# Turning x for the first stage: squares of 32 on VectorE and a way through DRAM in place of TensorE

## The chip, the cores and the metric

The kernel runs on one core of a Trainium2 chip. The metric is the device time of one execution in microseconds (us); a kernel's time is the median of several runs. The core's engines are TensorE (PE in the profile, its weight loads PEld), VectorE (DVE), ScalarE (ACT), GpSimd (POOL) and SyncE (SP), which issues nearly all the DMAs. Each engine works through its own instructions in a fixed order; an instruction that waits holds back all that stand behind it on its engine.

## The reference

```python
x = A_x                                   # 1 x 2048 x 576, float32
mod = (silu(c) @ w_mod).reshape(1, 6, 1, 576)
sa, ca, ga, sb, cb, gb = (mod[:, i] for i in range(6))
h = layernorm(x) * (1 + ca) + sa
q, k, v = heads(h @ A_wqkv)               # 32 heads of 18
pq, pk = phi(q), phi(k)                   # phi(t) = (t + 1 if t > 0 else exp(t)) + 1e-6
kv, z = einsum("bhsd,bhse->bhde", pk, v), einsum("bhsd->bhd", pk)
o = einsum("bhqd,bhde->bhqe", pq, kv) / (einsum("bhqd,bhd->bhq", pq, z) + 1e-6)
x = x + ga * (o @ A_wo)
h = layernorm(x) * (1 + cb) + sb
x = x + gb * (silu(h @ B_w1) @ B_w2)      # B_w1 576 x 4608
```

## The kernel before

The 2048 rows are 16 tiles of 128 rows, in four blocks (`tb` = 0 to 3) of four tiles. The first stage, about the first 205 us, makes k, v and half of q for all tiles and sums `kv` and `z` over them. The later stages (attention output, second layernorm, MLP) fill the remaining time and are the same instructions in both kernels.

A product with h needs h with its 576 columns on the partitions, that is, turned. So each block goes through these steps. `load_x` brings four tiles of x by DMA (L278, tiles `xt`). `LayerNorm.stats` (L190, L191), `finish` (L195, L196 on POOL, L199) and `normalise` (L205 on ACT, L207 on DVE) normalise the rows in place; `normalise` works twice per tile, since the last 64 columns are also written a second time, to columns 576 to 639. `turn(tb, k)` then turns chunk k, for k = 0 to 4 (four chunks of 128 columns, and a fifth that holds the last 64 columns twice): `transpose_chunk` issues four TensorE transposes of 128x128 (L228) into the PSUM bank `psT`, `modulate` (L213, ACT) scales and shifts from `psT` into `h32`, and `split_h` makes the two parts that the products read: `hT` high by a cast on ACT (L219), `hT` low by a subtraction on DVE (L135). `hT` has two buffers, one block each.

The loop over tiles t = 0 to 15 puts TensorE's work into this order, for tile t of block tb: `k_proj(t)`, a turned chunk, `v_proj(t)`, a turned chunk, `kv_mm(t - 1)`, `q_proj`, a turned chunk. The chunks of block tb + 1 are turned in tiles 2 and 3 of block tb, three and two of them; tile 0 of the next block is the first to read them. `q_proj` runs in tiles 1 to 7 (two of them in tile 1). I call the instructions of tile t for k, v and q: k3, v3, q3 and so on. TensorE's order is the order of the program.

The products for k, v and q go into a pair of PSUM buffers `psK` (`ps2`, two of them) in turn: k3, v3, q3, k4, ... So q3 can begin when k3's buffer has been read, and k4 when v3's has. k3 is read by ACT (`e`, L342) and DVE (`a`, L347); v3 by three pairs of ACT (`vx`, L599) and DVE (`vx`, L135) instructions.

The table `FIRST` names for DVE, ACT, POOL and SP the order of the first stage's instructions, and `arrange` fixes them in this order. `mod_piece` makes further rows of `mod` in the meantime from `w_mod` (L284 loads, L557 and L559 on DVE); its results are wanted in tiles 5 and 8. The weights of q wait in `accb[2]` and `accb[3]`, which are later the accumulators of blocks 2 and 3, until ACT and POOL have split them into `wq` (L327, L332, L334). Block 0 is handled apart, in halves (`turn_half` and L421 turn its tiles 2 and 3), in both kernels alike.

Of the kernel before, what the change touches and what calls it, by code (L numbers as in the profile page):

```python
# [9 lines left out]
F32 = mybir.dt.float32  # L10
# [6 lines left out]
P = 128  # L17
# [5 lines left out]
def kernel(ctx: ExitStack, tc, A_x, A_wqkv, A_wo, B_x, B_w1, B_w2, c, w_mod, out):  # L23
# [32 lines left out]
    def behind(instructions):  # L56

        with ExitStack() as order:
# [36 lines left out]

    FIRST = {
        "DVE": """
            2 1 4-5 0 3 6-7 9-10 8 11-23 26 24-25 28 27 29-30 43 31-38 40 44 46-47 39 45 48-49 41-42 51 50 53-54 52
            55 60 56 61-62 68 57 69 71-72 70 73-75 77-78 76 79-80 86-88 63-64 81 58 65 82 84 66 83 67 89 85 59 90
            148-149 91-92 150 93-94 96 95 151 97 152 98-100 153 101-105 107 106 108-111 125-126 128-129 127 130  # L100
            112-113 131-132 134-135 133 136-137 114-115 138-139 141 116 140 142 117-124 143-147 154 182-184 155-156
            185 158 157 186 159 162 160-161 187 222-225 163-165 226 166-167 169 168 170-173 192-193 195-196 194 197
            174 198-199 201-202 175 200 203-204 176-177 205-206 208 178 207 209 179-181 188-191 210-214 216 215 217
            220 218-219 221 227-228 230 229 231 234 232-233 235-258
        """,
        "Activation": """
            0-4 6-7 5 8-10 13 11-12 14-19 21 20 22-25 27 26 28-29 31 30 32 39-40 36 33 37 41-42 48 38 50 34 52 43-44
            46 58 45 47 49 51 59 53 60 54 56 55 57 61 35 62-63 65-66 64 67 70 68 71 69 72-75 77-78 76 79-80 82 81
            83-86 93 95 94 87 96 88-92 97-102 104-105 103 106 109-110 107-108 111-114 116-117 115 118-119 121 120
            122-125 132 134 133 126 135 127-131 136-139 141-142 140 143 146-147 144-145 148-150 152-153 151 154  # L110
            157-158 155-156 159-178
        """,
        "Pool": """
            0-1 3-4 2 6-7 5 8-20
        """,
        "SP": """
            0-33 38-42 47-49 34-37 50-56 43-46
        """,
    }

    def arrange(orders, start):
        for engine, text in orders.items():
            traced = [i for i in nc.cur_bb.bb.instructions[start:] if i.engine == getattr(mybir.EngineType, engine)
                      and not isinstance(i, (mybir.BassTilePoolBoundary, mybir.InstTileManualSchedule))]
# [14 lines left out]
    dram = ctx.enter_context(tc.tile_pool(name="dram", bufs=1, space=bass.MemoryType.DRAM))  # L139
# [5 lines left out]
    pa = tc.alloc_tile_pool(name="pa", bufs=1)  # L145
# [6 lines left out]
    cols = {n: const.tile([P, KC + 1, 2], F32, name=f"col_{n}") for n in ("a", "b")}  # L152
# [5 lines left out]
    accb = [accp.tile([P, 4, D], F32, name=f"acc{b}") for b in range(NB)]  # L158
# [4 lines left out]
    hT = [hTa.tile([P, 2 * KC + 2, 512], F32R, name="hT")]  # L163
# [13 lines left out]
    class LayerNorm:  # L177
# [23 lines left out]
        def normalise(self, i, xt, r, eng):  # L201
            for o, lo, hi in ((D, KC * P, D), (0, 0, D)):
                dst, src, rstd = xt[:, o : o + hi - lo], r[:, lo:hi], self.rstd[:, i : i + 1]
                if eng is A:
                    A.activation(dst, src, AF.Identity, bias=self.nm[:, i : i + 1], scale=rstd)  # L205
                else:
                    V.tensor_scalar(dst, src, self.mv[:, i, 0:1], rstd, op0=ALU.subtract, op1=ALU.mult)  # L207

    def modulate(ps, cidx, hT, col, h32, eng):

        shift, scale = col[:, cidx, 0:1], col[:, cidx, 1:2]
        if eng is A:
            A.activation(h32, ps, AF.Identity, bias=shift, scale=scale)  # L213
        else:
            V.tensor_scalar(h32, ps, scale, shift, op0=ALU.mult, op1=ALU.add)

    def split_h(ps, cidx, hT, col, h32):
        hi, lo = (cidx, KC + cidx) if cidx < KC else (2 * KC, 2 * KC + 1)
        return A.copy(hT[:, hi, :], h32), sub_hi(hT[:, lo, :], h32, hT[:, hi, :])  # L219

    def modulate_split(*chunk):

        modulate(*chunk, A)
        return split_h(*chunk)

    def transpose_chunk(xt, cidx, ps):
        for i in range(4):
            T.transpose(ps[:, i * P : (i + 1) * P], xt[i][:, cidx * P : (cidx + 1) * P], ident)  # L228
# [39 lines left out]
    def psT():  # L268
        t = psA.tile([P, 512], F32, name="psT")
        return t  # L270
# [2 lines left out]
        t = psA.tile([P, 2, 512], F32, name="psK", bufs=2)  # L273
        return t

    def load_x(tb, i):
        xt = pa.tile([P, DX], F32, name="xt", bufs=4)
        nc.sync.dma_start(xt[:, :D], x[(tb * 4 + i) * P : (tb * 4 + i + 1) * P, :])  # L278
        return xt

    def load_mod(dst, piece, k):
        kp = P if k < KC else 64
# [23 lines left out]
    xts = [load_x(0, i) for i in range(2)]  # L306
# [6 lines left out]
    xts += [load_x(0, i) for i in range(2, 4)]  # L313
    load_w(0, [KC])
    x0s = xts
    for j in (1, 2):
# [112 lines left out]
    def turn_half():  # L429

        pT = rooms(psT())
        turn_tiles(pT, (2, 3), START)
        for k in START:
            modulate_split(*half_args(1, k, pT))
# [194 lines left out]
        return ts  # L629

    def turn(tb, k):
        ps = psT()
        transpose_chunk(xts, k, ps)
        h32 = pa.tile([P, 512], F32, name="h32")
        modulate_split(ps, k, hT[tb], cols["a"], h32)

    QB = NT // 2
    qs = iter(range(NT))
    if True:
        for t in range(NT):  # L640
# [45 lines left out]
    with tc.manual_schedule(engines={mybir.EngineType.PE}):  # L686
# [4 lines left out]

        mp = pa.tile([P, DX], F32, name="xt", bufs=4)
# [10 lines left out]
        kvm = pa.tile([P, 2 * DX], F32, name="tmod")  # L705
        G.memset(kvm, 0.0)

        kvs = pa.tile([P, DX], F32, name="xt", bufs=4)[:, : NHC * HG].rearrange("p (j d) -> p j d", j=NHC)
        ku = pa.tile([P, DX], F32, name="xt", bufs=4)
# [40 lines left out]
        for j in range(KC + 1):  # L750
            psm = ps2()
            parts = [(cc, 0 if cc == j + 1 else 1) for cc in (j, j + 1) if cc < NHC]
# [7 lines left out]
            if j in (0, 2):  # L760
                r = rooms[j // 2]
# [806 lines left out]
```

## Time and profile before

| | |
|---|---|
| time, median of 3 runs | 1155.94 us (1155.23 to 1156.3) |
| the profiled execution | 1155.44 us, its span 1153.7 us |
| granted TensorE clock | 1.00 |
| TensorE busy | 1133.2 us, 98% of the span |
| VectorE busy | 974.8 us, 84% |
| ScalarE busy | 531.2 us, 46% |
| GpSimd busy | 658.3 us, 57% |
| TensorE transposes of x in blocks 1 to 3 (L228, `psT`) | 60, from 51.5 to 168.5 us |

Times in the profile run from the start of the span. A group's row names line, engine, operation, tiles (output<-inputs), shape and count, then busy time in all and the mean of one in ns, then the idle time of the engine before it and what ended it. A row of the timeline has start, length, engine, line, operation, tiles, shape and count.

### The profile page before, as it was taken

What the parts mean: (1) busy time and instruction counts of PE and PEld (TensorE: products, weight loads), DVE (VectorE), ACT (ScalarE), POOL (GpSimd) and SP (SyncE); (2) the same over time, 40 slices, a digit from 0 to 9 for tenths busy, and PEclk for the clock granted to TensorE, in tenths of its full rate; (3) what the DMA queues carried; (4) which work ended last, traced back from release to release, by engine and by line L of the source; (5) the groups of instructions that cost most, each with busy time, mean ns of one, the idle gap of its engine ahead of it and who ended that gap; (6) DMA issues with size and microseconds to landing.
All of it is one profiled execution on the core that took longest, in us unless ns stands there. A gap on an engine that the chain in (4) does not pass through costs nothing.

```text
span 1153.7 us, 19489 instructions
## 1 busy us (share of the span) xinstructions
PE 1133.2 (98%) x7159; PEld 1046.4 (91%) x7159; DVE 974.8 (84%) x1552; ACT 531.2 (46%) x1086; POOL 658.3 (57%) x748
## 2 busy tenths in 40 slices
PE   6999999999999999999999999999999999999998
PEld 4999999899998889999999999999999999999998
DVE  6876643577797999999999999999999999999996
ACT  4743442336655545444444444454454444444441
POOL 3300000264624686775776677667757767776786
PEclk9999999999999999999999999999999999999999
DMA  9522100123258976968869769779688697697674
GB/s 289 152 83 78 42 1 1 44 73 124 72 207 298 377 268 257 352 260 314 312 248 352 275 251 351 273 255 359 261 304 321 251 351 271 254 343 277 254 305 154
DMA packets 58318, 268.60 MB, mean 233 GB/s; under 512 B 5548, under 2 KB 21424, under 8 KB 35184
## 3 DMA queue, kind: packets, MB, share of 16 engines
q1 hardware_dynamic: 58052, 267.06, 63.3%
q8 instruction: 57, 0.93, 0.3%
q10 hardware_dynamic: 172, 0.30, 0.1%
q14 instruction: 37, 0.30, 0.1%
HBM read 250.56 MB, written 16.78 MB: 232 GB/s over the span
## 4 chain that ended last, share of the span: by engine, by line
PE 95%; DMA 3%; ACT 1%; DVE 1%; issue 0%; SPq 0%; ACTq 0%
PE up L1299 33%; PE down L1372 32%; PE psK L243 13%; PE big L243 7%; PE small L862 2%; PE big L873 2%; PE kvp L613 2%; DMA acc<-in_A_wqkv_dram 1%; DMA hT<-in_w_mod_dram 1%; PE psK L756 1%; PE big L788 1%; DMA room<-hd 1%; PE small L228 1%; PE psT L228 1%; PE up L1402 1%; PE down L1402 1%
## 5 line engine op out<-in xcount | busy, mean ns | idle before, releaser
L1380 DVE TENSOR_TENSOR acc<-down,acc 128x576 f32<-128x576 f32 x330 | 246.2, 753 | 14.1 <-PE down L1372 4.1
L1299 PE MATMUL up<-hT,w 128*128 128x512 f32 x916 | 240.3, 391 | 0.0
L1299 PEld LDWEIGHTS up<-hT,w 128*128 128x128 f32 x916 | 164.5, 188 | 25.7
L1334 POOL TENSOR_TENSOR s<-f,f 128x256 f32<-128x256 f32 x66 | 51.9, 786 | 163.9 <-ACT f L1315 163.9
L1372 PE MATMUL down<-w,hc 128*128 128x288 f32 x792 | 120.7, 294 | 0.0
L1372 PE MATMUL down<-w,hb 128*128 128x288 f32 x792 | 120.6, 294 | 0.0
L1372 PEld LDWEIGHTS down<-w,hb 128*128 128x128 f32 x792 | 113.6, 188 | 5.9 <-DVE U L1380 0.3
L1372 PEld LDWEIGHTS down<-w,hc 128*128 128x128 f32 x792 | 113.6, 188 | 5.6
L1380 DVE TENSOR_TENSOR U<-down,U 128x576 f32<-128x576 f32 x132 | 99.4, 753 | 17.9 <-PE down L1372 15.6
L135 DVE TENSOR_TENSOR w<-v,w 128x288 fp32r<-128x288 f32 (+1 forms) x170 | 111.7, 666 | 0.1
L243 PE MATMUL psK<-w,hT 128*128 128x256 f32 (+1 forms) x638 | 103.9, 298 | 0.0
L1299 PE MATMUL up<-room,w 128*128 128x512 f32 x348 | 93.2, 396 | 1.1 <-DMA room<-hd 1.1
L243 PEld LDWEIGHTS psK<-w,hT 128*128 128x128 f32 x638 | 91.7, 189 | 0.3 <-DVE acc L347 0.2
L1353 POOL TENSOR_TENSOR hc<-s,hc 128x512 fp32r<-128x512 f32 x66 | 89.5, 1355 | 0.0
L1315 ACT ACTIVATE f<-f 128x512 f32<-128x512 f32 x102 | 64.3, 631 | 47.8 <-DVE f L1320 25.4
L1318 DVE TENSOR_TENSOR f<-up,p 128x512 f32<-128x512 f32 x102 | 69.6, 683 | 14.7 <-PE up L1299 10.0
L196 POOL TENSOR_TENSOR rstd<-ve,neghalf 128x4 f32<-128x4 f32 (+3 forms) x10 | 9.7, 968 | 121.1 <-DVE ve L195 120.0
L1299 PEld LDWEIGHTS up<-room,w 128*128 128x128 f32 x348 | 62.4, 188 | 12.4 <-DVE f L1320 1.6
L1042 ACT CAST w<-v 128x288 fp32r<-128x288 f32 x85 | 36.6, 434 | 76.7 <-PE down L1372 55.2
L1338 POOL TENSOR_TENSOR f<-f,s 128x256 f32<-128x256 f32 x66 | 50.9, 771 | 34.1 <-DVE hb L1353 28.5
L1372 PE MATMUL down<-w,hd 128*128 128x288 f32 x396 | 63.2, 295 | 0.0
L1372 PE MATMUL down<-w,he 128*128 128x288 f32 x396 | 63.1, 295 | 0.0
(306 smaller groups left out, 2534.7 us busy)
## 6 DMA issues: line engine op xcount, KB each, us to landing
hT<-hd SPq DMA_DIRECT2D x66, 1280.0 KB, 5.9
hT<-hd SPq DMA_DIRECT2D x45, 1024.0 KB, 5.5
room<-hd SPq DMA_DIRECT2D x35, 1280.0 KB, 5.5
room<-hd SPq DMA_DIRECT2D x20, 1024.0 KB, 5.3
v<-in_B_w_dram SPq DMA_DIRECT2D x17, 576.0 KB, 6.9
v<-in_B_w_dram SPq DMA_DIRECT2D x17, 512.0 KB, 7.3
hd<-S SPq DMA_DIRECT2D x6, 1024.0 KB, 3.8
xt<-in_A_x_dram SPq DMA_DIRECT2D x16, 288.0 KB, 3.8
```

The lines of the kernel that those rows point to most:

```text
L135: return V.tensor_sub(lo, full, f32(hi))
L228: T.transpose(ps[:, i * P : (i + 1) * P], xt[i][:, cidx * P : (cidx + 1) * P], ident)
L243: T.matmul(ps, xpart(a), wpart(b), start=n == 0, stop=n == len(XW) - 1)
L1042: A.copy(self.w2[n][:, 0], src)
L1299: T.matmul(ps, left, right, start=first and m == 0, stop=m == len(seq) - 1, skip_group_check=True)
L1315: A.activation(self.f[i, k], self.f[i, k], AF.Silu)
L1318: V.tensor_add(f, self.bank[bank[1]], self.p1)
L1334: G.tensor_add(self.s[:, 0:1], half(i, 0, 1), half(i, 1, 1))
L1338: G.tensor_sub(half(i, 1, 0), half(i, 1, 0), self.s[:, 1:2])
L1353: eng.tensor_sub(t[:, :, 1, :], src, f32(t[:, :, 0, :]))
L1372: T.matmul(ps[:, p, :HALF], self.a[i, n][:, u, p * P : (p + 1) * P], self.w.w2[n][:, v], start=n in (1, 5, 7, 6) and j == 0, stop=j == 2, ...
L1380: V.tensor_add(dst, ps[:, :, :HALF], dst)
```

## The change

For blocks 1 to 3 TensorE's transposes go. The rows of a block are dealt anew: partition 32a + j of tile t holds row 128a + 32t + j (`load_block`, four DMAs of 32 partitions by 4 rows). `turn_block` turns each tile of the normalised block in squares of 32 on VectorE, into `sq`, which lies in `accb[3]`; four DMAs write `sq` to DRAM, 32 partitions each, in runs of 128 numbers (512 bytes); eight DMAs read it back with 2048-byte runs, four of 32 partitions by 4 runs into `xT` in `accb[2]` and four of 32 partitions by one run into the fifth chunk. `turn` then only modulates, in place, from SBUF, and splits as before. The block's four x tiles are one buffer. Block 1's load stands after `turn_half`, and the double 64 columns need no second normalisation. The orders of `FIRST` are new for DVE, ACT, POOL and SP.

```diff
     FIRST = {
...
-    def load_x(tb, i):
-        xt = pa.tile([P, DX], F32, name="xt", bufs=4)
-        nc.sync.dma_start(xt[:, :D], x[(tb * 4 + i) * P : (tb * 4 + i + 1) * P, :])
+    def rows4():
+        t = pa.tile([P, 4, DX], F32, name="xt")
+        return t
+
+    def load_x(i):
+        xt = x0[:, i]
+        nc.sync.dma_start(xt[:, :D], x[i * P : (i + 1) * P, :])
         return xt
+    def load_block(tb):
+        xx = rows4()
+        for a in range(4):
+            src = x[tb * 512 + a * P : tb * 512 + (a + 1) * P, :].rearrange("(t j) d -> j t d", t=4)
+            nc.sync.dma_start(xx[32 * a : 32 * a + 32, :, :D], src)
+        return xx
+
+    def turn_block(tb, xx):
+        sq = accb[NB - 1].rearrange("p a d -> p (a d)").rearrange("p (f q) -> p f q", q=P)
+        for t in range(4):
+            V.transpose(sq[:, :, 32 * t : 32 * t + 32], xx[:, t, :D].rearrange("p (f i) -> p f i", i=32))
+        room = dram.tile([32, D // 32, 4, P], F32, name=f"turned{tb}")
+        for a in range(4):
+            nc.sync.dma_start(room[:, :, a, :], sq[32 * a : 32 * a + 32])
+        xT = accb[NB - 2].rearrange("p a d -> p (a d)")[:, : KC * 512].rearrange("p (c q) -> p c q", c=KC)
+        tail = pa.tile([P, 512], F32, name="h32")
+        src = room.rearrange("i f a q -> i f (a q)")
+        for b in range(4):
+            nc.sync.dma_start(xT[32 * b : 32 * b + 32], src[:, b : 4 * KC : 4])
+        for b in range(4):
+            nc.sync.dma_start(tail[32 * b : 32 * b + 32], src[:, 4 * KC + b % 2])
+        return [xT[:, k] for k in range(KC)] + [tail]
...
     def turn(tb, k):
-        ps = psT()
-        transpose_chunk(xts, k, ps)
-        h32 = pa.tile([P, 512], F32, name="h32")
-        modulate_split(ps, k, hT[tb], cols["a"], h32)
+        modulate_split(xT[k], k, hT[tb], cols["a"], xT[k])
...
-            if i == 0 and more:
-                xts = [load_x(tb + 1, j) for j in range(4)]
+            if i == 0 and more and t > 0:
+                xx = load_block(tb + 1)
...
                 for j in range(4):
-                    ln.stats(j, xts[j])
+                    ln.stats(j, xx[:, j, :D])
                 ln.finish()
                 for j in range(4):
-                    ln.normalise(j, xts[j], xts[j], A if j % 2 else V)
+                    ln.normalise(j, xx[:, j], xx[:, j], A if j % 2 else V, ((0, 0, D),))
+                xT = turn_block(tb + 1, xx)
...
                 turn_half()
+                xx = load_block(1)
```

More of the change, by code (lines that the diff above doesn't have):

```diff
@@ L97 @@
         "DVE": """
[L98 to L102, printed above, removed]
@@ L103 @@
-            174 198-199 201-202 175 200 203-204 176-177 205-206 208 178 207 209 179-181 188-191 210-214 216 215 217
-            220 218-219 221 227-228 230 229 231 234 232-233 235-258
+            2 1 4-5 0 3 6-7 9-10 8 11-14 17 15 18 16 19 22 20-21 26 23-25 28 27 29 43-44 46-47 45 48-49 31-35 51
+            36-37 30 38 40 39 41-42 50 53-54 52 55 60 56 61 57 62 58 88 63 89 64 90 65-69 71-72 70 73-75 77-78 76
+            79-80 91 81-87 93 59 92 94-96 152 99-100 97 101 103-104 98 102 106 105 109 113 110 107 111 153 112 108
@@ new lines @@
+            127-128 130 114 131 115 129 132-134 136 116 137 117 135 138-139 154 119 118 120 140 155 121 141-143 122
+            144-146 156 124 123 157 125 147-148 126 149-151 158 186-187 196-197 199-200 159-160 198 161 201 162-163
+            202 164 203 165 205-206 188 166-167 204 207 169 208 168 173 177 189 209-211 170-171 212 172 174 213 175
+            214 176 215 190-191 228 178-179 229-231 180-185 192 222 226 232 193-194 227 195 236 216 240 217-221
+            223-225 233-235 237-239 241-264
@@ L105 @@
         """,
         "Activation": """
[L107 to L110, printed above, removed]
@@ L111 @@
-            157-158 155-156 159-178
+            0-4 6-7 5 8-10 13 11-12 14-17 21 18 20 29 31 19 30 32 22-25 27-28 26 41-43 39 36 33 40 37 48 50 38 34 52
+            44 46 45 47 56 49 57 51 58 53 35 59 54-55 60-61 65 62 66-67 70 63 68 64 71 69 75 73 80 72 76 81 77-79 74
+            82-87 91-92 88-89 93 90 94-98 100 105 99 101 108 102 106 103 112 104 117 109 113 118 107 128 110 129 111
+            114-116 119-124 135 140 125 136 142 141 146 151 126 143 147 127 152 130-134 137-139 144-145 148-150
@@ L112 @@
+            153-172
         """,
         "Pool": """
-            0-1 3-4 2 6-7 5 8-20
+            0-1 3-4 2 6-7 5 8-12 15-17 13-14 18-20
         """,
         "SP": """
-            0-33 38-42 47-49 34-37 50-56 43-46
+            0-33 62 34-45 63 46-49 64-66 71-72 50-53 67-70 54-57 73 58-61 74-75 88-91 76-87 92
         """,
@@ L123, in arrange @@
             traced = [i for i in nc.cur_bb.bb.instructions[start:] if i.engine == getattr(mybir.EngineType, engine)
-                      and not isinstance(i, (mybir.BassTilePoolBoundary, mybir.InstTileManualSchedule))]
+                      and not isinstance(i, (mybir.BassTilePoolBoundary, mybir.InstTileManualSchedule, mybir.InstRegisterMove))]
             before = None
@@ L199, in finish, with normalise @@
             V.scalar_tensor_tensor(nm, self.mv[:, a:b, 0], -1.0, rstd, op0=ALU.mult, op1=ALU.mult)
-        def normalise(self, i, xt, r, eng):
-            for o, lo, hi in ((D, KC * P, D), (0, 0, D)):
+        def normalise(self, i, xt, r, eng, parts=((D, KC * P, D), (0, 0, D))):
+            for o, lo, hi in parts:
                 dst, src, rstd = xt[:, o : o + hi - lo], r[:, lo:hi], self.rstd[:, i : i + 1]
@@ L304, in load_w @@
             load_rows(acc[5 * j + k], A_wqkv[:, ((j + 1) % 3) * D : ((j + 1) % 3 + 1) * D], k)
-    xts = [load_x(0, i) for i in range(2)]
+    x0 = rows4()
+    xts = [load_x(i) for i in range(2)]
     for a in range(2):
@@ L312 @@
     load_w(0, range(HEAD, KC))
-    xts += [load_x(0, i) for i in range(2, 4)]
+    xts += [load_x(i) for i in range(2, 4)]
     load_w(0, [KC])
@@ L689 @@
         kv_mm(NT - 1)
-        mp = pa.tile([P, DX], F32, name="xt", bufs=4)
+        rest = rows4()
+        mp = rest[:, 0]
         mask, pick = mp[:, :HG], mp[:, P : 2 * P]
@@ L706 @@
         G.memset(kvm, 0.0)
-        kvs = pa.tile([P, DX], F32, name="xt", bufs=4)[:, : NHC * HG].rearrange("p (j d) -> p j d", j=NHC)
-        ku = pa.tile([P, DX], F32, name="xt", bufs=4)
+        kvs = rest[:, 1, : NHC * HG].rearrange("p (j d) -> p j d", j=NHC)
+        ku = rest[:, 2]
         kvu = ku[:, : NHC * HG].rearrange("p (j d) -> p j d", j=NHC)
```

## The prediction

> **What bounds the kernel now.** I read the page's head, its chain, then the busy time by stretches of the first stage, since only that stage is changed.
>
> ```profile
> span 1153.7 us, 19489 instructions
> ...
> PE 1133.2 (98%) x7159; PEld 1046.4 (91%) x7159; DVE 974.8 (84%) x1552; ACT 531.2 (46%) x1086; POOL 658.3 (57%) x748
> ...
> PE 95%; DMA 3%; ACT 1%; DVE 1%; issue 0%; SPq 0%; ACTq 0%
> ...
> 35.00:75.00 40.00, 40.00 (x307) 39.79 (x306) 32.41 (x67) 22.12 (x46) 6.73 (x5) 1.00 0.52 155
> 75.00:126.00 51.00, 50.38 (x384) 49.82 (x383) 34.10 (x59) 19.53 (x37) 1.02 (x1) 1.00 0.17 46
> 126.00:170.00 44.00, 43.23 (x331) 42.86 (x330) 23.11 (x50) 19.38 (x37) 3.40 (x6) 1.00 0.08 27
> ```
>
> The last three rows give, after the length, the busy time of PE, PEld, DVE, ACT, POOL, then granted clock, DMA share and GB/s. TensorE has no idle time from 35 to 75 us and loses 0.6 and 0.8 us in the next two stretches, at the full clock. ACT is busy half of the time, DVE four fifths in the first stretch and about half in the third. So work taken from TensorE here is time, as long as nobody makes TensorE wait instead. Later stages are the same instructions with TensorE at 98% of the whole span; a shift of the first stage passes through to the end.
>
> **What goes.** The transposes are 60 instructions:
>
> ```profile
> L228 PE MATMUL psT<-ident,xt 128*128 128x128 f32 x60 | 9.0, 272 | 0.0
> ...
> 47.80 0.43 PE L243 MATMUL psK<-w,hT 128*128 128x288 f32 x2
> 75.03 0.43 PE L243 MATMUL psK<-w,hT 128*128 128x288 f32 x2
> 87.40 0.43 PE L243 MATMUL psK<-w,hT 128*128 128x288 f32 x2
> 102.73 0.51 PE L243 MATMUL psK<-w,hT 128*128 128x288 f32 x2
> 129.81 0.43 PE L243 MATMUL psK<-w,hT 128*128 128x288 f32 x2
> 150.23 0.43 PE L243 MATMUL psK<-w,hT 128*128 128x288 f32 x2
> 169.79 0.42 PE L243 MATMUL psK<-w,hT 128*128 128x288 f32 x2
> 187.17 0.43 PE L243 MATMUL psK<-w,hT 128*128 128x288 f32 x2
> ```
>
> 9.0 us is the time that they were in flight; what they cost is seen from the pace. The rows of the timeline are the starts of k2, k4, k5, k6, k8, k10, k12 and k14. A tile with q and no transposes (t = 4) takes 87.40 - 75.03 = 12.37 us. Tiles 2 and 3, with five chunks turned, take 27.23: 2.49 above two such tiles. Tiles 6 and 7 take 27.08: 2.34 above. Tiles 10 and 11 take 19.56 against 17.38 for tiles 12 and 13: 2.18. The sum is 7.0 us. The changed kernel's TensorE order is the old one without these 60, nothing added. That the change leaves them in is thus excluded.
>
> **What comes: DVE and ACT.** Per block DVE gets four turns of 128x576, and drops two normalisations of 64 columns; ACT drops two as well and now modulates from SBUF. No row shows such a turn.
>
> ```profile
> L207 DVE TENSOR_SCALAR xt<-xt,mv,rstd 128x576 f32<-128x576 f32 x6 | 3.3, 573 | 0.0
> L135 DVE TENSOR_TENSOR pk<-a,pk 128x576 fp32r<-128x576 f32 x16 | 12.3, 768 | 5.8 <-ACT pk L363 5.0
> L559 DVE SCALAR_TENSOR_TENSOR tmod<-raw,sc,tmod 128x1152 f32<-128x1152 f32 x6 | 8.5, 1414 | 0.1
> ```
>
> Bounds for one turn: 573 ns, the quickest row of that size, and 1414 ns, two passes of it. I take 768, a full pass between SBUF tiles. Twelve turns are 9.2 us of DVE time, beside TensorE where DVE has 7.6 us free of 40, 17 of 51 and 21 of 44. It counts only as a link in the chain below. ACT modulating from SBUF I leave at its old price (778 ns below); it can be no gain for TensorE.
>
> **What comes: a chain through DRAM.** In the old kernel a chunk goes from TensorE to `hT` in about 2 us. Now a block is loaded, normalised, turned, written and read back before anything of it can be modulated, and SP issues 16 further small DMAs per block less four old ones. The DMA rows:
>
> ```profile
> 69.97 1.75 SPq L278 DMA_DIRECT2D xt<-in_A_x_dram  x4
> ...
> xt<-in_A_x_dram SPq DMA_DIRECT2D x4, 288.0 KB, 4.8
> ...
> 12.57 0.55 SPq L249 DMA_DIRECT2D acc<-in_A_wqkv_dram  x1
> ...
> GB/s 184 251 218 251 218 218 201 302 352 302 218 168 218 251 184 151 218 235 218 302 302 419 385 419 352 419 386 402 385 402 402 352 386 318 251 184 151 235 251 218
> ```
>
> Four x loads of 288 KB on 128 partitions take 1.75 us to issue and 4.8 us (median) to land: the last starts about 1.4 us in and lands 5 to 6.2 us after the first issue. I take 5.3. The new transfers reach 32 partitions each, and the last row shows what fewer partitions do: it is the rate from 17.5 to 23 us in 40 slices. The first 20, in which the 64-partition loads (L249, L250) come through the queue behind one another, have a mean of 233 GB/s, the 14 after them, with 128 partitions, 381. I take 233 for 32 partitions too: 1.18 MB (4 x 288 KB) then takes 5.1 us instead of 3.1, the four main reads (1.05 MB) 4.5 instead of 2.8. So a load or a write is 5.3 + 2.0 = 7.3 us, the reads 5.3 - 0.3 + 1.7 = 6.7. The lower bound is 5.3 and 5.0, as with 128 partitions. The upper bound, from rows of 64 partitions at their slowest (151 GB/s), is 7.8 us of data instead of 5.1: 10.0 and 9.2.
>
> [...]
>
> **Block 1, link by link.** Rows for the links:
>
> ```profile
> 35.02 0.49 PE L421 MATMUL kvp<-ident,xt 128*128 128x128 f32 x3
> 71.30 3.89 PE L243 MATMUL psK<-wq,hT 128*128 128x288 f32 x28
> ...
> 73.07 1.53 DVE L190 BATCH_NORM_STATS2 st<-xt 128x6 f32<-128x288 f32 x4
> 74.52 0.32 DVE L191 BATCH_NORM_AGGREGATE mv<-st 128x2 f32<-128x12 f32 x2
> ...
> L196 POOL TENSOR_TENSOR rstd<-ve,neghalf 128x4 f32<-128x4 f32 x3 | 3.0, 1011 | 91.3 <-DVE ve L195 91.3
> ...
> L213 ACT ACTIVATE h<-psT,col_a 128x512 f32<-128x512 f32 x15 | 11.7, 778 | 0.2
> L219 ACT CAST hT<-h 128x512 fp32r<-128x512 f32 x15 | 9.3, 621 | 0.4
> L342 ACT ACTIVATE e<-psK 128x576 f32<-128x576 f32 x23 | 15.0, 652 | 54.8 <-PE psK L243 54.8
> L599 ACT CAST vx<-psK 128x252 fp32r<-128x252 f32 x30 | 11.0, 367 | 17.8 <-PE psK L243 11.1 <-DVE vx L135 6.6
> ...
> L135 DVE TENSOR_TENSOR vx<-psK,vx 128x252 fp32r<-128x252 f32 x30 | 12.5, 418 | 11.2 <-ACT vx L599 11.2
> L351 DVE SCALAR_TENSOR_TENSOR a<-e,a 128x576 f32<-128x576 f32 x16 | 12.1, 757 | 0.5
> L135 DVE TENSOR_TENSOR vx<-psK,vx 128x72 fp32r<-128x72 f32 x14 | 3.2, 232 | 4.1 <-ACT vx L599 4.1
> ```
>
> The block's buffer is free when block 0's last tiles have been turned (35.02 + 0.49 = 35.5). Load 7.3: 42.8. Statistics of four tiles, 2 x 1.78 (73.07 to 74.84, twice): 46.4. Variance, POOL's power (1.01) and mean: 1.4, so 47.8. Two normalisations on DVE (ACT's two beside them): 1.1, 48.9. Four turns at 768 less 0.08 overlap each: 2.8, 51.7. Write 7.3: 59.0. Reads 6.7: 65.7, which I call M.
>
> Now what stands behind it. In the new orders ACT has after the reads: modulate 0 and 1, cast 0, modulate 2, cast 1, modulate 3, `e` of k3, modulate 4, casts 2 to 4, then the first `vx` of v3. DVE has the low parts 0 and 1 before `a` of k3, then low parts 2 to 4, then v3's `vx` three times with `a` (757) and one `tmod` (1414) among them. So k3's buffer is read only about M + 5.2 (four modulates, two casts, `e`, `a`), and v3's at M + 10.3: on ACT 5 x 0.778 + 5 x 0.621 + 0.652 + 0.367 = 8.0, less 0.9 for overlap of records, then on DVE 0.418 + 0.757 + 0.418 + 1.414 + 0.232, less overlap, 3.2 with the hand-overs. TensorE, freed of block 1's 2.5 us, would begin q3 at 71.30 - 2.5 = 68.8 and k4 at 75.03 - 2.5 = 72.5. q3 needs k3's buffer (70.9: 2.1 late), k4 needs v3's (76.0: 3.5 late, the first delay included). Block 1 thus loses 3.5 of its 2.5 gained.
>
> **Blocks 2 and 3** have a tile more between load and use. Block 2's turns end in tile 5 at about 93, its write 100.4; the load of block 3 is issued before the reads and goes through the queue first (5.1), so the reads land near 110. `e` of k6 is done near 108, modulates 0 to 2 then stand before v6's `vx`, which ends near M2 + 5.8 = 116; k7 wants that buffer at 116.0. Block 3: turns until 127, M3 = 127.2 + 14.0 + 0.7 = 142; ACT's copy of `bc_gb` stands behind two modulates and ends at 144, when v9 wants its buffer. So both are just covered, at nothing; if a chain is one microsecond longer, each of the three blocks costs one more. `tmod` has its two results later than before, but well ahead of tile 5 and 8. The start (0 to 35 us) is reordered on DVE, ACT and POOL; ACT's second pair of normalisations now stands before casts of block 0's last chunks. I put 0, between -0.5 and +1.
>
> **Sum.** -7.0 + 3.5 = -3.5 us on the profiled execution's own 1155.44 (span 1153.7 and 1.7 around it), which lies 0.5 under the median: 1151.9. What a measurement of this kernel can tell from no change is about 0.2%, 2.3 us.
>
> **Rivals.** (1) The 32-partition transfers run as those on 128 (5.3, 5.3 and 5.0): the load lands at 40.8, M = 61.7 with DVE free of block 0 near 42.5, and k4 is just in time, all 7.0 stay: 1148.4. [...] Against: the dips to 233. (2) Slower: the chain through DRAM is the bound of all three blocks. It decides from the point where the chains are 1.2 us longer than I take: 3.5 + 3 x 1.2 = 7. With turns of 1414 ns (4 x 0.65 = 2.6) the loss is 3.5 + 3 x 2.6 = 11.3, the time 1159.7. [...] For it: three trips in a row, none seen so far with 512-byte runs. Against: DVE rows of that size end below 768. (3) In between, chains 0.4 to 1.9 longer: no change, 1153.1 to 1157.6.
>
> **The numbers.** Forecast, 1149.5 to 1153.1 by itself: 0.42. Rival 1: 0.18. Rival 3: 0.17. Rival 2: 0.23. Faster is the first two, 0.60. The range goes from 1148.0 (rival 1 with a little gained at the start) to 1158.5, which leaves out most of rival 2.
>
> **What the changed profile would show.** No `psT` row from the L228 helper before 200 us. One turn on DVE near 0.77 us. The last write of block 1 landing about 7 us after the first issue, near 59, its reads near 66. TensorE waiting twice in block 1, at q3 for DVE's `a` of k3 and at k4 for DVE's `vx`, 3.5 us together, and not in blocks 2 and 3. Tiles 6 and 7 then take 24.7 us, tiles 10 and 11 17.4. Wrong would be: waits of TensorE near tiles 7 and 9, turns above 1 us, or a time outside the range.

## The result, and the profile after

The changed kernel takes 1160.0 us (median of 5 runs, 1159.55 to 1160.45), the kernel before 1155.7 beside it (5 runs): a ratio of 1.0034, 95% interval 1.0022 to 1.0045. It is slower by 0.3%, little but clear of the noise, where I forecast 1151.9 in 1148.0 to 1158.5. The profiled execution took 1160.45 us.

The page of the changed kernel, its head and its chain:

```profile
span 1158.7 us, 19443 instructions
...
PE 1129.1 (97%) x7099; PEld 1040.9 (90%) x7099; DVE 981.3 (85%) x1558; ACT 527.3 (46%) x1080; POOL 659.0 (57%) x748
...
PE 88%; DMA 4%; DVE 4%; ACT 2%; SPq 1%; issue 1%; POOL 0%; ACTq 0%; DVEq 0%
```

The 60 transposes are gone (7159 - 7099) and TensorE is busy 4.1 us less. But its share of the chain falls from 95 to 88%: DVE, DMA and ACT now stand on the path. The busy time by stretches (columns as in the prediction) and the starts of k2, k4, k5, k6, k8, k10, k12 and k14 in the timeline follow; what stands in square brackets behind a row is the idle time of the engine before it and what ended it.

```profile
35.00:75.00 40.00, 36.90 (x278) 36.38 (x278) 25.75 (x55) 20.45 (x42) 7.51 (x5) 1.00 0.65 151
75.00:126.00 51.00, 47.79 (x356) 46.81 (x355) 40.00 (x79) 18.34 (x35) 3.38 (x2) 1.00 0.64 166
126.00:170.00 44.00, 40.20 (x297) 38.98 (x295) 27.62 (x48) 17.65 (x35) 2.33 (x5) 1.00 0.30 74
...
49.45 0.43 PE L244 MATMUL psK<-w,hT 128*128 128x288 f32 x2
78.52 0.50 PE L244 MATMUL psK<-w,hT 128*128 128x288 f32 x2 [1.25 <-DVE vx L136]
91.01 0.43 PE L244 MATMUL psK<-w,hT 128*128 128x288 f32 x2
106.34 0.51 PE L244 MATMUL psK<-w,hT 128*128 128x288 f32 x2
134.42 0.50 PE L244 MATMUL psK<-w,hT 128*128 128x288 f32 x2 [0.51 <-DVE vx L136]
156.74 0.43 PE L244 MATMUL psK<-w,hT 128*128 128x288 f32 x2
174.71 0.43 PE L244 MATMUL psK<-w,hT 128*128 128x288 f32 x2
192.05 0.43 PE L244 MATMUL psK<-w,hT 128*128 128x288 f32 x2
```

TensorE lacks 3.1, 3.2 and 3.8 us of busy time in the three stretches; before it lacked 0.0, 0.6 and 0.8. Against the starts before: k2 is 1.65 later. Tiles 2 and 3 take 29.07 where two tiles without transposes take 24.74, 4.3 lost; tiles 6 and 7 take 28.08, 3.3 lost; tiles 8 and 9 take 22.32 against 20.42 before, 1.9 lost; tiles 10 and 11 take 17.97 against 17.38, 0.6 lost. k14 is 4.88 later, and the span is 5.0 longer, so nearly all of it is lost before k14.

What TensorE waited for is in the view of waits (total, times, longest), and one more row of the timeline tells of the start:

```profile
PE psK L244 <- DVE vx L136: 3.4, 4, 1.3
PE psK L244 <- DVE a L379: 2.1, 2, 1.5
PE psK L244 <- ACT bc_gb L606: 1.3, 1, 1.3
PE psK L605 <- DVE col_b L600: 1.0, 1, 1.0
PE psK L244 <- DVE acc L379: 0.8, 1, 0.8
...
11.37 0.69 PE L453 MATMUL psK<-ident,xt 128*128 128x128 f32 x2 [1.40 <-DVE xt L208]
```

In the three blocks it never waits for `hT`, the data that make the detour. It waits for buffers in PSUM whose readers on ACT and DVE stand behind the work on the turned chunks. The way through DRAM itself, in the changed kernel (DMA issue on SP, then the first modulates on ACT; the last two rows give the issue times of one DMA in ns, smallest, median, largest):

```profile
L299 DVE STREAM_TRANSPOSE acc<-xt 128x576 f32<-128x576 f32 x12 | 8.7, 754 | 0.0
...
37.24 1.77 SPq L292 DMA_DIRECT2D xt<-in_A_x_dram  x4
53.47 3.91 SPq L302 DMA_DIRECT2D turned<-acc  x4
61.06 1.74 SPq L307 DMA_DIRECT2D acc<-turned  x4
67.93 1.52 ACT L214 ACTIVATE acc<-acc,col_a 128x512 f32<-128x512 f32 x2 [4.12 <-DMA acc<-turned]
102.79 1.91 SPq L307 DMA_DIRECT2D acc<-turned  x4
114.69 1.52 ACT L214 ACTIVATE acc<-acc,col_a 128x512 f32<-128x512 f32 x2 [3.63 <-DMA acc<-turned]
142.71 1.75 SPq L307 DMA_DIRECT2D acc<-turned  x4
149.61 1.52 ACT L214 ACTIVATE acc<-acc,col_a 128x512 f32<-128x512 f32 x2 [4.57 <-DMA acc<-turned]
...
L302 SPq DMA_DIRECT2D turned<-acc x12: 566/864/1416, 53.5 to 137.4; - x12
L307 SPq DMA_DIRECT2D acc<-turned x12: 310/423/607, 61.1 to 144.0; - x12
```

### The profile page after: what moved, and what is told of

The parts are those of the page before. It is cut to its first block, busy times and chain, and to the rows that moved or that the text cites. A ratio compares the mean times of both kernels' runs of the same rounds, so it can differ in the third digit from the quotient of the medians.

```text
span 1158.7 us, 19443 instructions
## 1 busy us (share of the span) xinstructions
PE 1129.1 (97%) x7099; PEld 1040.9 (90%) x7099; DVE 981.3 (85%) x1558; ACT 527.3 (46%) x1080; POOL 659.0 (57%) x748
## 4 chain that ended last, share of the span: by engine, by line
PE 88%; DMA 4%; DVE 4%; ACT 2%; SPq 1%; issue 1%; POOL 0%; ACTq 0%; DVEq 0%
PE up L1331 33%; PE down L1404 32%; PE big L244 7%; PE psK L244 6%; PE small L894 2%; PE big L905 2%; DMA acc<-turned 2%; PE kvp L645 1%; PE psK L788 1%; PE psK L472 1%; ACT acc L214 1%; PE big L820 1%; DMA room<-hd 1%; PE small L229 1%; DMA hT<-in_w_mod_dram 1%
## 5 line engine op out<-in xcount | busy, mean ns | idle before, releaser
L197 POOL TENSOR_TENSOR rstd<-ve,neghalf 128x4 f32<-128x4 f32 (+3 forms) x10 | 10.6, 1058 | 102.2 <-DVE ve L196 101.0
```

## The experiments

My theory after the result: the data come in time, but late enough that ACT and DVE, which work in a fixed order, stand in modulates and low parts while PSUM wants to be read. The rival: the way through DRAM is itself too long. Each row was timed beside the kernel before (1156.0 to 1156.5 in these runs); all ratios are to it.

| run | what | us | ratio, 95% interval |
|---|---|---|---|
| e1 | order of the start | 1160.8 | 1.0044, 1.0030 to 1.0059 |
| e2 | orders of blocks 1 to 3 | 1158.6 | 1.0025, 1.0014 to 1.0035 |
| e3 | both | 1157.4 | 1.0007, 0.9995 to 1.0019 |
| e4 | block 3's load after block 2's reads | 1166.6 | 1.0094, 1.0079 to 1.0109 |
| e5 | loads and reads on 128 partitions, outer dimension 4 | 1192.2 | 1.0312, 1.0295 to 1.0329 |
| e6 | e3, further | 1157.0 | 1.0007, 0.9998 to 1.0016 |
| e7 | e6 and e5 | 1183.0 | 1.0231, 1.0216 to 1.0246 |
| e8 | no way through DRAM | 1152.5 | 0.9963, 0.9949 to 0.9977 |
| e9 | each read a whole chunk | 1154.1 | 0.9979, 0.9967 to 0.9991 |
| e10 | e9 and more orders | 1159.6 | 1.0024, 1.0011 to 1.0036 |
| e11 | the same orders alone | 1161.4 | 1.0050, 1.0035 to 1.0065 |
| e12 | e9, orders of the start and block 1 | 1149.5 | 0.9941, 0.9928 to 0.9953 |
| e13 | e12, loads on 128 partitions | 1149.6 | 0.9948, 0.9935 to 0.9962 |
| e14 | e9, loads on 128 partitions | 1155.1 | 0.9990, 0.9978 to 1.0002 |
| e15 | the orders of e12 alone | 1162.5 | 1.0048, 1.0032 to 1.0064 |
| e16 | e9 with one read for all chunks | 1156.3 | 0.9997, 0.9986 to 1.0008 |

### Orders alone: e1 to e4

e1, in `FIRST`, DVE (15 and 16 are L208 of the first tile, 17 and 18 sums of modulation rows):

```diff
-11-14 17 15 18 16 19 22
+11-12 14-16 13 17-19 22
```

> The changed kernel, with only VectorE's order of the start altered: the mean and the two normalisations of block 0's first tile stand ahead of the sums of modulation rows, which wait for their DMA at 9.19 us. Theory (order of the start): the first transposes start near 9.4 instead of 11.37 us and k2 near 47.8 instead of 49.45; 1.6 us less, 1158.4. Rival (the chains through DRAM bound the three blocks, and they do not start earlier): the 1.6 us are lost again at k4, 1159.5 to 1160.5.

k2 comes at 47.76 (before: 47.80), so in these two executions the 1.65 us of the start go with this order. k2 moves between executions, though: without e5, e7 and e10, it comes at 48.70 to 50.72 with the changed kernel's order of the start, at 47.38 to 48.86 with e1's. TensorE's wait for `xt` is 1.40 us in the changed kernel and 0.6 in e2; e1 and e3 have none. The time doesn't follow: the reads are issued 1.5 us earlier, but the first modulate comes 0.2 earlier, and q3 waits longer. From the timeline of e1:

```profile
59.53 1.74 SPq L307 DMA_DIRECT2D acc<-turned  x4
67.70 1.52 ACT L214 ACTIVATE acc<-acc,col_a 128x512 f32<-128x512 f32 x2 [5.65 <-DMA acc<-turned]
73.05 5.52 PE L244 MATMUL psK<-wq,hT 128*128 128x288 f32 x28 [3.05 <-DVE a L379]
```

The reads took 8.2 us here against 6.9. Over the runs with the reads into 32 partitions and the old loads it was 6.9 in the changed kernel and e4, and 8.2 to 8.8 in e1, e2, e3, e6, e11 and e15. The rate is nearly the same, 201 and 203 GB/s from issue to modulate in the first two, 211 to 220 in the others; but 1.4 MB pass in that time in the first two and 1.7 to 1.9 MB in the others. The surplus comes in rows of 4608 bytes (0.06 MB of them pass in the changed kernel), the length of a row of `w_mod`'s load, which is issued behind the reads. Why more of it passes beside them there is open. The last row shows something more: q3's 28 matmuls take 5.52 us, where 3.99 followed a wait of 1.52. The rival's time came true.

e2, the reads of PSUM moved ahead (ACT and DVE, block 1 as an example, then the same in blocks 2 and 3):

```diff
 ACT, block 1
-63 68 64 71 69 75 73 80 72 76 81 77-79 74
+73 63 68 64 71 77 69 78 72 79 75-76 80-81 74
 DVE, block 1
-98 102 106 105 109 113 110 107 111 153 112 108
+106-107 98 110 102 111-112 105 109 113 108 153
```

On ACT 73 is `e` of k3, 77 to 79 are `vx` of v3, 63, 68, 71, 75 and 80 the modulates.

> The changed kernel, with only the orders of ScalarE and VectorE in blocks 1 to 3 altered: the reads of a k, v or q result in PSUM stand ahead of the modulates, casts and low parts of the turned chunks, and ahead of the turns and normalisations that are not due; the DMAs and their order are unchanged. Theory (TensorE waits for PSUM buffers whose readers stand behind the turned chunks' work): the waits before q2 (0.81), q3 (1.52), k4 (1.25), k7 (1.35), q7 (0.62), k8 (0.51) and v9 (1.32) go, 7.4 us: 1152.6; no row of TensorE waits for hT. Rival (the way through DRAM is itself too long): TensorE waits for hT at k4, k8 or k12 in place of the buffers, the gain is under 2.5 us, 1157.5 or more.

> Both edits, that of the start and that of blocks 1 to 3. Theory (order): the sum, 1.6 + 7.4 = 9.0 us less than 1160.0: 1151.0, faster than the kernel before by about 4.7. Rival (way through DRAM): TensorE reaches block 1's turned chunks earlier and waits for hT at k4; 1156 or more.

(The wait of 0.81 is v2's, for the buffer of a q; I misnamed it.) The waits named went, but for k4's (1.20 in e2, 1.10 in e3) and k8's (0.75), and no row of TensorE waits for `hT`. In e3 tiles 6 and 7 take 25.80 us instead of 28.08, so for blocks 2 and 3 the theory holds. By the time, though, both runs fell where the rival had put them (1157.5 or more, 1156 or more). For a new wait came before v4: on DVE q3's reader, at 79.59 in e3, now stands behind a `tmod` and statistics of block 2, which run from 77.17 on. TensorE waits 2.89 us, and behind it the granted clock falls. The windows of e3:

```profile
79.00:80.39 1.39, 0.00 (x0) 0.00 (x1) 1.39 (x4) 0.00 (x0) 0.00 (x0) 1.00 0.43 83
80.39:82.00 1.61, 1.61 (x6) 1.61 (x7) 1.61 (x6) 0.00 (x0) 0.00 (x0) 0.50 0.36 126
82.00:84.00 2.00, 2.00 (x10) 2.00 (x10) 2.00 (x5) 0.00 (x0) 0.00 (x0) 0.55 0.05 8
84.00:86.00 2.00, 2.00 (x17) 2.00 (x16) 1.97 (x5) 0.70 (x2) 1.06 (x1) 1.00 0.00 0
```

The third column from the right is the granted clock: 0.50 for 3.4 us after a pause of 2.9. That cost about another 1.9 us: tile 4 took 17.16 instead of 12.37, of which 2.89 are the pause. A shorter pause had such a stretch behind it too: 1.80 us in e4 (before v9, at 157.04; the clock is at 0.50 from 158.5 to 161.9).

e4, SP:

```diff
-50-53 67-70 54-57 73 58-61
+50-61 73 67-70
```

> The changed kernel, with only SyncE's order altered: block 3's load of x is issued after block 2's reads of the turned chunks instead of between the writes and the reads. Theory (order of the readers): block 2's reads land 5 us earlier (near 110 instead of 114.7), the modulates come before v6 is done, k7's wait of 1.35 goes, and block 3's load comes 6 us later, which moves its turns against other readers: 1157.5 to 1160. Rival (way through DRAM, with the queue in front of it, is the bound): blocks 2 and 3 lose 5.8 us against the forecast through this queue, and most of block 2's 3.3 comes back: 1156.5 to 1157.

Both were wrong. Block 2's reads do land earlier (the first modulate at 110.94 instead of 114.69), but block 3's statistics stand ahead of k6's reader on DVE and wait for the load that now comes later; q6 waits for it, and the clock falls again (0.50 from 120.19 to 124). A row of e4:

```profile
120.19 5.86 PE L244 MATMUL psK<-wq,hT 128*128 128x288 f32 x28 [4.93 <-DVE a L379]
```

### The transfers: e5 to e9, e16

e5 leaves all orders. Loads by tile, reads by chunk:

```diff
-            src = x[tb * 512 + a * P : tb * 512 + (a + 1) * P, :].rearrange("(t j) d -> j t d", t=4)
-            nc.sync.dma_start(xx[32 * a : 32 * a + 32, :, :D], src)
+        src = x[tb * 512 : (tb + 1) * 512, :].rearrange("(a t j) d -> t a j d", a=4, t=4)
+            nc.sync.dma_start(xx[:, t, :D], src[t])
...
-            nc.sync.dma_start(xT[32 * b : 32 * b + 32], src[:, b : 4 * KC : 4])
+            nc.sync.dma_start(xT[:, c], src[:, 4 * c : 4 * c + 4].rearrange("i b w -> b i w"))
```

> The changed kernel with its orders untouched; the same bytes in the same runs, but each of the four x loads of a block (rows of 2304 bytes) and each of the four main reads (runs of 2 KB) reaches all 128 partitions instead of 32; a read then brings one whole chunk. Theory (a transfer on 32 partitions is slow as such): load 2.0 us and reads 1.7 us shorter, the first modulate of block 1 near 63 instead of 67.9, waits before q3, k4 (2.77) and k7 (1.35) gone: 1154 to 1156. Rival (the number and length of the runs sets the rate, all 16 DMA engines being busy already): the last byte lands as before, and only what comes of the first chunk's earlier landing is gained: 1158 to 1160.

Far off on the other side. A window of e5 in which the loads run, DMA share and GB/s last:

```profile
41.00:43.00 2.00, 2.00 (x18) 2.00 (x18) 1.43 (x3) 1.63 (x6) 0.17 (x1) 1.00 0.23 90
```

A quarter of the DMA engines' time is used, at 90 GB/s; the old loads keep them all busy at about 200 (in the changed kernel a share of 1.05 and 218 GB/s in the same window). The source's outer dimension here is 4, and I took that for the cause. How the transfer was spread over the engines, no view shows; but in e9 and e14 transfers into 128 partitions with an outer dimension of 128 have none of this (e14's loads run at 330 to 401 GB/s).

e6 and e7 have the start's order, and orders that go further than e2's (82 is `e` of q3):

```diff
 ACT, block 1
-63 68 64 71 69 75 73 80 72 76 81 77-79 74 82
+73 77 63 78 64 79 68-69 71-72 82 75-76 80-81 74
```

> The kernel with both orders altered, with more of the same: the reads of v3, q3 and k4 also stand ahead of the modulates and of the statistics of block 2, which wait for x, and so on in blocks 2 and 3; DMAs untouched. Theory (order): the wait before v4 (2.89) goes, and with it the stretch at half the granted clock behind it (1.7 us): 1157.4 - 4.6 = 1152.8, at best 1151.5 with k4's wait gone too. Rival (way through DRAM): TensorE then waits for hT at k4 and v4, 1155.5 or more.

> The orders of the run before with the transfers on 128 partitions. If block 1's chain still sets k4: 1 to 2 us less than with the order alone, 1150 to 1151.5. If the order alone covers the chain: the same as that one within 0.5 us.

e6 did half: the waits before k4 and v4 were gone. But what the rival had said came in their place: the first modulate came at 69.6, 8.8 us after the issue, so TensorE waited for `hT` itself in k4 (0.64 us at 77.18 for ACT's cast, and shorter waits around it), and tile 4 took 15.27 us, 2.9 more than without. A `tmod` ahead of q7's reader made v8 wait 2.18. e7 carries e5's loads and tells no more.

e8 leaves out the four writes and eight reads of each block; the modulates take the squares in SBUF:

```diff
-        room = dram.tile([32, D // 32, 4, P], F32, name=f"turned{tb}")
...
+        wide = sq.rearrange("p f q -> p (f q)")
+        return [wide[:, 512 * k : 512 * k + 512] for k in range(KC)] + [wide[:, 14 * P : 18 * P]], tail
```

> The changed kernel with its orders untouched and the way through DRAM left out: the four writes and eight reads of each block are gone, and the modulates take the turned squares as they lie in SBUF, in other places than the reference wants. Theory (only the order of the readers behind late modulates costs): with the data there at once the waits before q3, k4, k7, v9 go, the start's 1.65 and the wait before q2 (0.81) stay: 1154 to 1155.5. Rival (VectorE's turns and the new load take the time, not the way through DRAM): 1158 or more.

Between 50 and 140 us two waits are left, 0.92 (v2) and 0.62. With the same orders and turns, 7.5 us went, more than the theory's 4.5 to 6: it is the way through DRAM, by the waits the lateness of its data, that makes the orders wrong. That the turns or the load on DVE cost the time is excluded.

e9 lays the room out so that a chunk is 128 rows of 2 KB in one piece:

```diff
-        room = dram.tile([32, D // 32, 4, P], F32, name=f"turned{tb}")
+        room = dram.tile([D // 32, 32, 4, P], F32, name=f"turned{tb}")
-            nc.sync.dma_start(room[:, :, a, :], sq[32 * a : 32 * a + 32])
+            nc.sync.dma_start(room[:, :, a, :].rearrange("f i q -> i f q"), sq[32 * a : 32 * a + 32])
-        src = room.rearrange("i f a q -> i f (a q)")
+        src = room.rearrange("f i a q -> (f i) (a q)")
-            nc.sync.dma_start(xT[32 * b : 32 * b + 32], src[:, b : 4 * KC : 4])
+            nc.sync.dma_start(xT[:, c], src[c * P : c * P + P])
```

> The changed kernel with its orders and its x loads untouched. The room in DRAM is laid out by square and row of the square, so that each of the four main reads brings one whole chunk, 128 rows of 2 KB that lie behind one another, to all 128 partitions; the writes keep their runs of 512 bytes. Theory (a read into 32 partitions is slow as such): the four reads land at over 300 GB/s, the first modulate of block 1 comes 3 us after the issue instead of 6.9, near 64, and the waits before q3, k4 and k7 go: 1155.5 to 1157. Rival (any read of this size goes at 220 GB/s): the first modulate comes some 3 us earlier, by the chunk's smaller share, the last chunk as before: 1157 to 1159. [...]

Faster than the kernel before, and below the theory's range. Block 1 in e9:

```profile
60.33 1.76 SPq L307 DMA_DIRECT2D acc<-turned  x4
63.25 1.51 ACT L214 ACTIVATE acc<-acc,col_a 128x512 f32<-128x512 f32 x2
66.36 0.82 ACT L214 ACTIVATE acc<-acc,col_a 128x512 f32<-128x512 f32 x1 [1.09 <-DMA acc<-turned]
```

The first modulate comes 2.9 us after the issue instead of 6.9, but the third waits until 66.4. So much of it isn't a faster transfer: each old read brought a quarter of the partitions of every chunk, so that the first modulate needed all four; now it needs one. In blocks 2 and 3 only the waits are left that the kernel before has as well (0.62, and 1.04 for `col_b` against 0.8); block 1 keeps v2's 0.92, k4's 1.70 and v4's 0.36.

e16 parts the two: one read in place of four, into the same 128 partitions.

```diff
-            nc.sync.dma_start(xT[:, c], src[c * P : c * P + P])
+        nc.sync.dma_start(xT, src[: KC * P].rearrange("(c p) w -> p c w", p=P))
```

> The ninth run with its four reads of one chunk each made one read of all four chunks: the same room, the same 512 runs of 2 KB into 128 partitions, but nothing can be modulated before all of it has landed. Theory (the ninth run gained by the chunks' landing one after the other; its last chunk landed no sooner than the changed kernel's): the first modulate of block 1 comes 6 to 7 us after the issue, as in the changed kernel, and the time is near the changed kernel's, 1158 to 1160. Rival (128 partitions read faster): the first modulate comes 4 to 5 us after the issue, 1155 to 1156.5.

```profile
61.33 0.38 SPq L306 DMA_DIRECT2D acc<-turned  x1
67.60 1.52 ACT L214 ACTIVATE acc<-acc,col_a 128x512 f32<-128x512 f32 x2 [3.23 <-DMA acc<-turned]
139.54 0.39 SPq L306 DMA_DIRECT2D acc<-turned  x1
145.18 1.52 ACT L214 ACTIVATE acc<-acc,col_a 128x512 f32<-128x512 f32 x2 [3.58 <-DMA acc<-turned]
```

6.3 us from issue to modulate in block 1, as the theory said, and 5.6 in block 3, where the changed kernel took 6.9 and 6.9. The time, though, is the rival's. About 4 us of the 6 come with reads whose last byte lands 0.6 to 2.7 us sooner after the issue (block 2: 9.2 against 11.9), about 2 with the chunks landing one by one; by the ratios it is 4.3 and 2.1, and in the traces k14 starts at 192.05 in the changed kernel, 187.57 in e16 and 185.62 in e9. Both count, and I had given the first too little. Its cause isn't single, though: e16 reads into 128 partitions, but also with one DMA in place of four, and its issue ends 1.4 us sooner (0.38 us in place of 1.74). e9, with four DMAs into 128 partitions, has its last main read of block 1 landed 7.1 us after the first issue, no sooner than the changed kernel's 6.8, with more of `w_mod`'s load beside it (1.56 MB in all against 1.38); in block 2 its third read lands after 8.8 us instead of 10.6. What the 128 partitions alone are worth in a read is thus not shown.

### Orders and transfers together: e10 to e15

e10 and e11 go on from e6, for example with q7's reader (178) on DVE; e10 has e9's reads as well:

```diff
-213 189 214-215 190-191 228 178
+212-214 178 215 189 179 190-191
```

> Both orders altered (the sixth run's, with v6's, q6's and q7's readers moved further ahead of the statistics and modulation rows that delayed them), and the reads of the run before. Theory (order and the reads of block 1 together are all that was lost): every wait over 0.7 us between 50 and 142 us goes, TensorE takes the 24.7 us for two tiles that the forecast gave: 1149.5 to 1151. Rival (something else is lost each time that one wait goes): 1153 or more.

> The same orders with the changed kernel's own DMAs. Theory: blocks 2 and 3 as in the run before; in block 1 the first modulate comes at 68 to 69.5 and TensorE, at k4 by 72.4, waits 2 us for hT as in the sixth run: 1152 to 1153. Rival (way through DRAM costs in every block): 1155 or more.

Both lost against the runs they go on from, e9 and e6, and the rivals' times came. In e11 k9 starts at 147.0, later than in the changed kernel: in tile 8 k8's reader and `col_b` now stand behind other work (waits of 2.00 us at 141.3 and 2.70 at 145.4, the clock at 0.50 behind them). e10's one trace is of an execution of 3949.9 us, from which the others can't be read; where it lost is open.

e12 alters only what e9 still waits for: the start as in e1, q1's reader between the turns, `col_b` ahead of v8's second part, and block 1:

```diff
 ACT, block 1
-63 68 64 71 69 75 73 80 72 76 81 77-79 74 82
+63 68 64 71 69 73 75 72 76-77 80 78 81 79 74 82
 DVE, block 1
-98 102 106 105 109 113 110 107 111 153 112 108 127-128 130 114 131 115 129
+98 102 106-107 105 109-111 113 112 108 114 153 115 127-128 130-131 129
```

> The wide reads of the ninth run, the start's order of the first, and in block 1 alone the reads of q1's, k3's, v3's and q3's results ahead of the turned chunks' last modulate and casts and ahead of block 2's statistics; blocks 2 and 3 keep the changed kernel's order, but col_b is read ahead of v8's second part. Theory (what is left is the start, 1.65, q1's wait 0.92, k4's 1.70, v4's 0.36 and some of col_b's 1.04): 1154.1 - 4.5 = 1149.6, 1149 to 1151. Rival (a wait removed comes back as another, as in the runs before with more altered): 1153 or more.

1149.5 us, as worked out: 6.8 less than the kernel before beside it. Its page, stretches and waits:

```profile
PE 95%; DMA 3%; DVE 1%; ACT 1%; issue 0%; POOL 0%; SPq 0%; ACTq 0%
...
35.00:75.00 40.00, 39.93 (x304) 39.70 (x302) 28.70 (x60) 21.27 (x44) 6.16 (x4) 1.00 0.66 162
75.00:126.00 51.00, 50.38 (x379) 49.62 (x377) 43.67 (x86) 20.29 (x38) 3.38 (x2) 1.00 0.62 169
126.00:170.00 44.00, 43.74 (x329) 43.21 (x328) 24.78 (x43) 17.11 (x34) 2.88 (x5) 1.00 0.23 62
...
PE psK L598 <- DVE acc L379: 0.6, 1, 0.6
PE psK L605 <- DVE col_b L600: 0.3, 1, 0.3
```

TensorE has 95% of the chain again and no wait that the kernel before lacked. k4 - k2 is 25.14 us, k8 - k6 25.02, k12 - k10 17.34: 6.4 us less than before, near the 7.0 of the transposes.

e13 and e14 bring rows 4p + t to partition p, on 128 partitions; the turn writes with a step of four:

```diff
+        src = x[tb * 512 : (tb + 1) * 512, :].rearrange("(p t) d -> t p d", t=4)
+            nc.sync.dma_start(xx[:, t, :D], src[t])
-            V.transpose(sq[:, :, 32 * t : 32 * t + 32], xx
+            V.transpose(sq.rearrange("p f (j t) -> p t f j", t=4)[:, t], xx
```

> The same, and the x loads of blocks 1 to 3 bring rows 4p + t to partition p, 128 partitions with an outer dimension of 128; the turns then write with a step of four, so that the columns come out in the order of the rows. If the load's 32 partitions were as slow as the reads': block 1's statistics start 1.5 to 2 us earlier, and its chain with them; since the orders already cover that, the time is within 1 us of the run before, 1148.5 to 1150.5. If a turn with a step of four takes longer than 0.77 us, VectorE gives it back: 1151 or more.

> The changed kernel's own orders with loads and reads on 128 partitions, both with an outer dimension of 128. Theory (32 partitions are slow, and the fifth run was slow only because its transfers had an outer dimension of 4): M is 2 us earlier than with the reads alone, k4's wait of 1.70 shrinks, 1152 to 1153.5. Rival (loads on 128 partitions are themselves slow here): 1155 or more.

A load lands in 4.2 us instead of 6.0 (median of the two of block 1's that the traces tell of, e14 against e9), but a turn takes longer. e14's group:

```profile
L299 DVE STREAM_TRANSPOSE acc<-xt 128x576 f32<-128x576 f32 x12 | 13.6, 1207 | 0.0
```

4 x 0.45 = 1.8 us are given back, so the times stay where they were (1149.6 against 1149.5). e14's 1155.1 is above its theory's 1152 to 1153.5 and no better than e9. The rival's time came, but not its reason, since the loads did land sooner: k4's wait fell from 1.70 to 0.29, but v2's, behind the turns, rose from 0.92 to 1.60, and k8 waits 0.89 anew.

e15, the orders of e12 with the old reads:

> The orders of the twelfth run (start, block 1, col_b) with the changed kernel's own DMAs: the fourth corner of the square of orders and reads. If the two add up: the orders gave 1154.1 - 1149.5 = 4.6 us beside the ninth run's reads, so 1160.0 - 4.6 = 1155.4. If they cover for each other, as where late reads hold ScalarE's modulates and all that stands behind them: block 1 still loses 2 to 3 us and blocks 2 and 3 their 5, 1157 or more.

They don't add up. The same orders that give 4.7 us beside e9's reads give nothing beside the old ones: 1162.5 is 2.5 more than the changed kernel's, though the ratios, 1.0048 and 1.0034, overlap in their intervals (in the traces k14 comes 2.8 later). `e` of k3 stands behind three modulates, the reads take 8.3 us here, so that the first comes at 69.2, and q3 waits 4.28 us and then runs at half the clock (0.50 until 78):

```profile
73.92 6.06 PE L244 MATMUL psK<-wq,hT 128*128 128x288 f32 x28 [4.28 <-DVE a L379]
```

## Why the prediction was wrong

**Right: the gain.** 7.0 us for the transposes; e12 has 6.4 of them in the tiles concerned, and TensorE's order adds nothing.

**Right: block 1's links.** A turn takes 0.754 us (taken: 0.768). Load 7.6, write 7.6, reads 6.9 against 7.3, 7.3 and 6.7. The reads landed at 67.9; less the start's 1.65 that is 66.3 against M = 65.7. TensorE waited at q3 (1.52) and k4 (1.25), for the buffers and through the engines named: 2.8 together, where I had 3.5. The loss was 4.3: v2 waited 0.81 for the reader of a q behind the turns, which I had not looked for, and 0.7 stand in none of the waits listed (e12's 25.14 has 0.4 of the kind). That the sum comes near is in part luck.

**Wrong: "the start ... I put 0".** k2 came 1.65 us later, outside my -0.5 to +1. I looked at ACT's casts; the delay came from DVE, where sums that wait for DMA (1.45 us, until 9.19) stand ahead of the first tile's normalisations (e1), and TensorE waited 1.40 for these.

**Wrong: blocks 2 and 3 "just covered, at nothing".** This step decided the case: it cost 3.3 and 1.9 + 0.6 us, 5.8 of the 8 us or so by which the kernel is slower than I forecast. I had the reads land near 110 and M3 at 142; they landed at 114.7 and 149.6. In block 2 SP took 3.83 us to issue four writes and 4.01 for the load behind them, and the reads, issued at 102.8 (I had 100.4), needed 11.9 us behind that load, where I had 9.6. I had priced issue by rows of 128 runs (0.44 us); a write of 576 runs took 0.57 to 1.42 here. In block 3 the turns ended at 135.0, not 127. Block 2's late reads had a hand in it: ACT stood idle for them 3.63 us before 114.69, DVE behind ACT 3.98 us before 116.81, in the middle of block 3's statistics. I said myself that each microsecond more would cost one per block, and took a cover of zero as a cover.

**The rivals.** Rival 2's time, 1159.7, is the measured one within 0.3, but by luck, since its condition isn't what happened: block 1's chain was 0.5 us longer than taken, not 1.2; blocks 2 and 3's reads landed some 5 and 8 us later than taken. Rival 1 asked whether the way becomes as quick as on 128 partitions: e14 has that for loads and reads (the writes still leave from 32), with the changed kernel's orders, and is near the kernel before rather than at 1148.4: the start's delay remains, waits of 1.60, 0.89 and 1.21 us before v2, k8 and for `col_b` too, and its turns are 0.45 us longer each.

**Right: the rate.** The 233 GB/s that I took for 32 partitions is near what came: 32-partition reads ran at 207 to 242 GB/s (226 to 238 in the changed kernel between 62 and 68 us). The loads did take longer into fewer partitions (6.0 us into 32 in e9, 4.2 into 128 in e14); for the reads e16 leaves it open, as said there. What I had not seen is the other cause, that each read carried a part of every chunk (2.1 us by the ratios of e16 and e9).

## What to carry to other kernels

When work leaves the bounding engine for a longer way round, ask first in which order the waiting engines stand: a result that is in time may still hold up, on an engine with a fixed order, the readers of a buffer that the bounding engine wants next. Cut transfers so that the first consumer needs only the first one. An order fits one set of arrival times (e12 against e15); change transfers first and orders after, and alter only what the trace still shows waiting (e12), since wider reorderings each brought a new wait.

## What I had not expected of the hardware

- Every wait of TensorE of 2.40 us or more between 45 and 200 us of these traces (among them 2.40 and 4.28 in e15, 2.70 in e11, 2.89 in e3, 3.05 in e1, 4.93 in e4) left it at a granted clock of 0.50 for 3.4 to 6.0 us of the work behind it, by estimate (half of that time) 1.7 to 3.0 us more each. Below that it went both ways: waits of 1.80 (e4) and 2.17 us (e7) were followed by 3.4 us at 0.50, waits of 1.78 (e1) and 2.18 us (e6) were not.
- A DMA whose outer dimension is 4 moved 90 GB/s at a DMA share of 0.23 (e5's loads); the same bytes and runs with an outer dimension of 32 about 200 (218 at a share of 1.05 in the changed kernel, 41 to 43 us).
- A turn of 128x576 that writes with a step of four took 1207 ns (e14), one without 754 (the changed kernel).
- In the changed kernel the issue of a write of 576 runs held SP for 0.57 to 1.42 us, that of a read of 128 runs for 0.31 to 0.61. The number of runs alone does not give it: an x load of 128 runs took 0.31 to 1.37 there, e16's read of 512 runs 0.38 to 0.39.
